# Two FFT convolutions in a written-out tile order: first-channel-group products beside other tiles, one list of spectrum slots, a ring of ten

## The chip, the core and the metric

The kernel runs on one core of a Trainium2 chip. The metric is device time in microseconds (us) from the first to the last instruction; the kernel before takes 455.67 us (median of 3 runs, 454.72 to 457.34). Six engines matter here: PE is the tensor engine, ACT the scalar engine, DVE the vector engine, POOL the GpSimd engine, SP the queue that issues nearly all transfers, and the DMA engines carry them. SBUF is the working memory, PSUM the accumulators that PE writes and that ACT or DVE must empty ("evacuate").

## The reference

Four residual layers follow one another on a 2048 x 512 activation: attention A, convolution B, attention A, convolution B. A is a sliding dilated attention (32 heads of 16, eight keys two positions apart). B is a long convolution along the sequence, with a kernel K made of complex exponentials, computed by FFT:

```python
K  = jnp.einsum("dn,dnl,dn->dl", Cc, P, dB).real     # (512, 2048)
Kf = rfft2(pad(K));  Uf = rfft2(pad(u.T))            # length 4096
Yf = Uf * Kf
y  = irfft2(Yf)[:, :, 0, :L].astype(bf16).T + u * Dskip
x  = x + _A(_layernorm(x));  x = x + _B(_layernorm(x))   # twice
```

Both B layers use the same K, so its spectrum is computed once, in the first convolution, and written to device memory for the second.

## The kernel before, in words

The program generates K on chip (`k_gen`), runs the first attention, the first convolution, the second attention and the second convolution. Only the two convolutions change.

The FFT is done by matrix products in two steps each way. The 512 channels are handled as 128 groups of four, split into two halves g = 0 and g = 1 of 64 groups each (`NG`, `DQG`). Class `FftB` has these pieces, each of which works on one PSUM tile of 128 x 1024 f32 (two of the eight banks):

- `f1` (line 697): first forward step. Sixteen half-width matmuls (line 706) fill a tile, and one evacuation writes it to `a1s`. There are eight tiles per half and source, t = 0 to 7. Sources are `ka` (the kernel K, first convolution only) and `ua` (the activation).
- `f2` (line 709): second forward step, sixteen 128 x 64 matmuls (line 713), eight tiles ("slots", ec = 0 to 7) per half and source. It reads all of `a1s` of its half.
- `k_f2` (line 716): an f2 tile of K, evacuated into a slot buffer and stored to `kf_dram` (line 729).
- `u_f2` (line 770): an f2 tile of the activation, evacuated by ACT into `ub` (line 776). `ub` has three buffers.
- `u_mult` (line 749): the spectral product of one slot, two DVE multiplications (line 757) of `ub` with the slot's spectrum kn and with its copy ks, in which real and imaginary rows are swapped. They write `t1` and `t2`.
- `i1` (line 780): first inverse step, sixteen matmuls (lines 791 and 792) that read `t1` and `t2` of a half over all eight slots, so each i1 tile needs all products of its half; the evacuation writes `z` (for g = 0 it is placed in the buffer `xnT`).
- `i2` (line 796): second inverse step, eight matmuls of 256 columns (lines 807 and 808), four tiles per half. With "dve" the residual is added by DVE (line 811); with "act" PE adds it by four more matmuls with the identity (line 806) and ACT copies; "both" splits the tile.

The spectrum copies come by DMA. In the first convolution `kf_load` (line 731) copies a slot's kn to its ks with even and odd partitions exchanged, two transfers inside SBUF. In the second it reads a slot from `kf_dram` in three transfers (lines 744 and 746), 512 KB in all, into a ring of seven slots. A slot is loaded again only after the product that used it.

The order of work in these stages is the program's order: a manual schedule is on for DVE, ACT, PE and SP, so each engine executes its instructions as they are recorded. `forward` (line 820) records in steps s: the product of the slot before, one f1 tile, and, eleven steps behind, one f2 tile. So all products come after the whole of K's spectrum, each directly after its u tile; after the eleventh of them i1 tiles of half 0 are put in between. `middle` (line 853) then records i1 of half 1 and i2 of half 0, and the main function records i2 of half 1. Which engine evacuates is decided by `evac` (line 690), a running balance: ACT is charged 0.93 and DVE 1.2 per tile, and the one with the smaller sum takes it.

PSUM for the convolutions is four tiles, two pools of two buffers (line 664), taken two and two in turn. After `middle`, `swap_psum` closes both and opens one pool of two buffers, and the other half goes to the next attention's front (transposes and key projections).

The two convolutions differ at the edges. Before the first, the list `late` of the attention (line 504) holds five pieces, among them the row statistics of `x_sb` rows 14 and 15 and the layer norm of the last rows; `forward` places one after each f1 tile. After the first, the next attention's front is recorded in the main function (lines 1312 to 1344): per block b of four row groups, `stats(b)` takes row statistics of the second channel half (four DVE instructions, line 91), `aggr`, `power` and `norm` produce `xn`, PE transposes it (line 205) into `pt`, ACT and DVE copy it to `xnT` (line 208), and `keys` project it. The statistics of the first channel half of block t are taken in `middle`, after `i2(0, t)`.

Of the kernel before, what the change touches and what calls it, by code (L numbers as in the profile page):

```python
# [20 lines left out]
P = 128  # L21
S = 2048
D = 512
# [20 lines left out]
EV = dict(act=0.93, dve=1.2)  # L44
# [96 lines left out]
class LayerA:  # L141
# [388 lines left out]

    def close_logits(self):
        self.lctx.close()
# [122 lines left out]
class FftB:  # L655


    def __init__(self, tc, nc, C, ident, w2_dram, g2_dram, kf_dram, x_sb, tag):
        self.tc, self.nc, self.C, self.ident, self.kf_dram, self.x_sb = tc, nc, C, ident, kf_dram, x_sb
        self.w2_dram, self.g2_dram = w2_dram, g2_dram  # L660
        self.tag = tag
        self.c_grp, self.c_mid, self.c_ps = ExitStack(), ExitStack(), ExitStack()
        self.grp = self.c_grp.enter_context(tc.tile_pool(name=f"b{tag}_grp", bufs=5, reuse_waits="tile"))
        self.ps = [self.c_ps.enter_context(tc.tile_pool(name=f"b{tag}_ps_{side}", bufs=2, space=PSUM, side=side))
                   for side in ("right", "left")]
        self.npt = 0
        self.load = dict(act=0.0, dve=0.0)
        self.pend = None
        g2p = self.c_grp.enter_context(tc.tile_pool(name=f"b{tag}_g2", bufs=1, reuse_waits="tile"))
        self.g2 = g2p.tile([P, 2, 16, P], BF16, name="g2_sb")  # L670
        self.S = [dict() for _ in range(NG)]

    def open_mid(self):
        tc, nc, t = self.tc, self.nc, self.tag
        nc.sync.dma_start(self.g2[:], self.g2_dram[:])
        self.kf_ring = None
        if self.ring_pool is None:
            self.ring_pool = self.c_mid.enter_context(tc.tile_pool(name=f"b{t}_kf", bufs=1, reuse_waits="tile"))
        self.ring2 = self.c_mid.enter_context(tc.tile_pool(name=f"b{t}_kf2", bufs=1, reuse_waits="tile")) if t else None
        self.nkf = 0  # L680
        self.wk = self.c_mid.enter_context(tc.tile_pool(name=f"b{t}_wk", bufs=3, reuse_waits="tile"))

# [7 lines left out]
    def evac(self, dst, src, eng=None):  # L690
        nc, load = self.nc, self.load
        if eng is None:
            eng = "act" if load["act"] + EV["act"] <= load["dve"] + EV["dve"] else "dve"
        load[eng] += EV[eng]
        (nc.scalar.copy if eng == "act" else nc.vector.tensor_copy)(dst, src)  # L695

    def f1(self, g, u, key, t):
        nc, C = self.nc, self.C
        if t == 0:
            self.S[g][key] = self.gtile("a1s", [P, P, DQG])  # L700
        a1s = self.S[g][key]
        p1 = self.ptile([P, DQT, P])
        for j in range(DQT):
            lhs = u[:, g * DQG + t * DQT + j].rearrange("p a r -> p (a r)")
            for half, m in enumerate((C["F1c"], C["F1s"])):
                nc.tensor.matmul(p1[half * 64:(half + 1) * 64, j, :], lhsT=lhs, rhs=m[:], start=True, stop=True)  # L706
        self.evac(a1s[:, :, t * DQT:(t + 1) * DQT], p1[:].rearrange("p q e -> p e q"))
# [8 lines left out]
    def k_f2(self, g, ec):  # L716
        if (g, ec) == (0, 0):
            self.nat = list(self.spare)
        elif ec == 0:
            kp2 = self.ring_pool.tile([P, 8, DQG, EC], BF16, name="kf_nat", tag="kp")  # L720
            self.kf_ring = kp2
            self.nat += [kp2[:, 4 + i] for i in range(4)]
        p2 = self.f2(g, "ka", ec)
        n = g * NEC + ec
        if n >= len(self.nat):
            self.nat.append(self.wk.tile([P, DQG, EC], BF16, name="kf_sb")[:])
        kf = self.nat[n]
        self.evac(kf, p2)
        self.nc.sync.dma_start(self.kf_dram[g, ec].rearrange("p r q e -> (p r) (q e)"), kf.rearrange("p q e -> p (q e)"))

    def kf_load(self, n):

# [7 lines left out]
        if self.kf_ring is None:  # L740
            self.kf_ring = [pool.tile([P, 4 - i, 2, DQG, EC], BF16, name=f"kf_ring{i}")
                            for i, pool in enumerate((self.ring_pool, self.ring2))]
        kc = self.kf_ring[n % 7 // 4][:, n % 7 % 4]
# [5 lines left out]
    def u_mult(self):  # L749

        if self.pend is None:
            return
        g, ec, ub = self.pend
        self.pend = None
        kn, ks = self.kf.pop(g * NEC + ec)
        for t, k in zip(self.S[g]["t"], (kn, ks)):
            self.nc.vector.tensor_tensor(t[:, :, ec * EC:(ec + 1) * EC], ub[:], k, ALU.mult)  # L757
        self.load["dve"] += 1.22
        n = g * NEC + ec
        if self.tag == 0:  # L760
            self.free += [ks] + ([kn] if n < len(self.spare) else [])
            more = len(self.free)
        else:
            more = 1
        while more and self.nkf < min(NG * NEC, n + 9):
            self.kf_load(self.nkf)
            self.nkf += 1
            more -= 1

    def u_f2(self, g, ec):  # L770
# [4 lines left out]
        ub = self.wk.tile([P, DQG, EC], BF16, name="ub")  # L775
        nc.scalar.copy(ub[:], p2)  # L776
        self.load["act"] += EV["act"]
        self.pend = (g, ec, ub)

    def i1(self, g, t, eng=None):  # L780
# [15 lines left out]
    def i2(self, g, t, eng="dve", defer=False):  # L796
# [12 lines left out]
        if n_add:  # L809
            xr = x_sb[:, t * 4:t * 4 + n_add, dsl]  # L810
            nc.vector.tensor_tensor(xr, p4[:, 0:n_add], xr, ALU.add)
            self.load["dve"] += 0.3 * n_add
        if n_add < 4:
            ev = lambda: nc.scalar.copy(x_sb[:, t * 4 + n_add:t * 4 + 4, dsl], p4[:, n_add:4])
            self.load["act"] += 0.23 * (4 - n_add)
# [4 lines left out]
    def forward(self, srcs, late=()):  # L820

        F1 = [(g, u, key, t) for key, u in srcs for g in range(NG) for t in range(NQT)]
        F2 = [(key, g, ec) for key, _ in srcs for g in range(NG) for ec in range(NEC)]
        lag = NQT + 3
        late = list(late)
        self.kf = {}
        n_u = 0
        for s in range(len(F2) + lag):
            self.u_mult()
            if s < len(F1):  # L830
                self.f1(*F1[s])
            if s > 0 and late:
                late.pop(0)()
            if s >= lag:
                key, g, ec = F2[s - lag]
                if s == max(lag, lag + len(F2) - NG * NEC - 4):
                    if self.tag == 0:
                        self.free = [self.kf_ring[:, i] for i in range(4)]
                    for n in range(self.ahead):
                        self.kf_load(n)  # L840
                    self.nkf = self.ahead
                if key == "ka":
                    self.k_f2(g, ec)
                else:
                    self.u_f2(g, ec)
                    n_u += 1
                    if n_u > NEC + 3:
                        self.i1(0, n_u - NEC - 4)
        self.u_mult()
        for t in range(NEC - 3, NQT):  # L850
            self.i1(0, t)

    def middle(self, done, eng=None, last="dve"):
        self.i1(1, 0, eng)
        self.i1(1, 1, eng)
        for t in range(NA // 4):
            if t == 3:
                self.i1(1, 6, eng)
                self.i1(1, 7, eng)
            self.i2(0, t, "dve" if t < 3 else last)  # L860
            done(t)
            if t < 2:
                self.i1(1, 2 + 2 * t, eng)
                self.i1(1, 3 + 2 * t, eng)

    def swap_psum(self):
        self.c_ps.close()
        self.c_ps = ExitStack()
        self.ps = [self.c_ps.enter_context(self.tc.tile_pool(name=f"b{self.tag}_ps2", bufs=2, space=PSUM))]
# [317 lines left out]
def kernel(  # L1187
# [93 lines left out]
    fb.free = None  # L1281
    fb.open_mid()
    with tc.manual_schedule(engines=MAN):
        fb.forward((("ka", kp), ("ua", u)), late)
# [4 lines left out]
    with tc.manual_schedule(engines=MAN):  # L1289
        fb.middle(lambda t: half_stats(nc, lnst, x_sb, t, 0), "act", "act")  # L1290
# [4 lines left out]
        def stats(b):  # L1295
            half_stats(nc, lnst, x_sb, b, 1)

# [14 lines left out]
        fb.i2(1, 0)  # L1312
# [53 lines left out]
    fb.ahead = 7  # L1366
    fb.open_mid()
    with tc.manual_schedule(engines=MAN):
        fb.forward((("ua", u),))
    fb.c_mid.close()  # L1370
    la.close()
    out_v = out.rearrange("b (p a) d -> p (b a) d", p=P)

    def store(g):
        gs = slice(g * 4 * DQG, (g + 1) * 4 * DQG)

        def rows(t):
            for a in ((t * 4, t * 4 + 2) if (g, t) == (1, 3) else (t * 4,)):
                a1 = a + (2 if (g, t) == (1, 3) else 4)
                nc.sync.dma_start(out_v[:, a:a1, gs], x_sb[:, a:a1, gs])  # L1380
        return rows

    with tc.manual_schedule(engines=MAN):
        done = store(0)
        fb.middle(done)
        done = store(1)
        for t, eng in enumerate(("dve", "act", "dve", "both")):
            fb.i2(1, t, eng)
            done(t)
# [32 lines left out]
```

## Time and profile before

| what | from the page or an answer of the trace |
|---|---|
| span | 453.2 us, 12714 instructions |
| PE busy | 354.9 us (78%), weight loads 268.0 us (59%) |
| DVE busy | 402.2 us (89%) |
| ACT busy | 326.0 us (72%) |
| transfers | 54.17 MB, mean 120 GB/s |
| mean granted PE clock | 0.980 |
| first convolution | about 213 to 286 us: DVE busy 60.5, ACT 60.7, PE 63.5 of 73.0 us |
| second convolution | about 396 to 452 us: DVE busy 42.0, ACT 40.0, PE 44.4 of 56.0 us |

Busy shares are averages over stages with different limits. In both convolutions no engine is busy all the time, and what a change of order is worth must be read from who waits for whom: an engine that waits holds back what stands behind it in its queue. Busy time of PE contains overlapping matmuls, so a busy PE isn't PE at its peak. A busy sum that is built of long runs also counts a small overlap at the seams: an ACT evacuation lasts 1.02 us, but in an unbroken run they start 0.9 to 0.93 us apart.

### The profile page before, as it was taken

The page shows a single profiled execution, that of the slowest core. Times are in us where ns is not written, and L with a number is a line of the kernel's source. Part 1 is how long each engine was busy: PE and PEld are TensorE (multiplying, and loading weights), DVE is VectorE, ACT ScalarE, POOL GpSimd, SP SyncE. Part 2 cuts the span into 40 slices and gives each one's busy share as a digit, 9 for nine tenths or more (in the row PEclk, how much of TensorE's full clock was granted, in tenths as well). Part 3 has the DMA queues.
Part 4 walks back from the last instruction along what each step waited for, and adds up shares of the span by engine and source line. Part 5 has one row for each costly group of instructions (what it writes and reads, how often), then busy time and mean ns, then how long its engine had stood idle before and what let it go on. Part 6 is the DMA issues. An engine that isn't in the chain of part 4 may idle for free.

```text
span 453.2 us, 12714 instructions
## 1 busy us (share of the span) xinstructions
PE 354.9 (78%) x5459; PEld 268.0 (59%) x5498; DVE 402.2 (89%) x558; ACT 326.0 (72%) x543; POOL 44.5 (10%) x46
## 2 busy tenths in 40 slices
PE   1000065888999989989898788999999899996885
PEld 1000034666676667767787787555657687776874
DVE  6799999999899999898897888889999999878964
ACT  5979979576555559967999886774654559699943
POOL 2000110100089300000400000000000020000000
PEclk9999997899999999999999999999999999998999
DMA  8920730121411575480266440670033053016714
GB/s 213 391 80 12 79 66 19 32 64 24 101 16 43 160 234 159 135 338 14 112 245 221 176 169 7 173 249 1 2 82 83 1 213 161 18 79 184 239 48 140
DMA packets 65354, 54.17 MB, mean 120 GB/s; under 512 B 36781, under 2 KB 53778, under 8 KB 64018
## 3 DMA queue, kind: packets, MB, share of 16 engines
q1 hardware_dynamic: 65154, 53.22, 38.8%
q8 instruction: 43, 0.70, 0.7%
q10 hardware_dynamic: 144, 0.13, 0.3%
q14 instruction: 13, 0.11, 0.1%
HBM read 30.28 MB, written 13.24 MB: 96 GB/s over the span
## 4 chain that ended last, share of the span: by engine, by line
PE 52%; ACT 20%; DVE 16%; DMA 7%; issue 3%; SPq 1%; DVEq 0%; ACTq 0%
PE po L385 9%; PE pp L219 6%; PE pq L326 6%; PE pq L162 5%; PE L L280 5%; PE pq L397 4%; PE pk L1111 4%; DVE t L757 4%; DVE pav L377 3%; ACT a1s L695 3%; DMA v_ext<-v_ext 3%; PE pb L713 2%; PE pb L706 2%; ACT ln_junk L86 2%; ACT ln_junk L81 2%
## 5 line engine op out<-in xcount | busy, mean ns | idle before, releaser
L377 DVE TENSOR_TENSOR pav<-attn,v_ext 128x4096 bf16<-128x4096 bf16 x32 | 72.7, 2282 | 0.5 <-DMA v_ext<-v_ext 0.5
L273 DVE TENSOR_TENSOR prod<-qT,kT_ext 128x4096 bf16<-128x4096 bf16 x29 | 66.2, 2299 | 1.1 <-ACT qT L164 0.6
L385 PEld LDWEIGHTS <-pav 128*128 128x128 bf16 x1024 | 58.6, 98 | 13.0 <-DVE pav L377 9.4
L385 PE MATMUL po<-ident,pav 128*128 128x128 bf16 x1024 | 62.5, 219 | 4.8 <-DVE pav L377 4.8
L205 PE MATMUL pt<-ident,x_blk 128*128 128x128 bf16 x64 | 5.6, 241 | 45.1 <-ACT x_blk L136 45.1
L791 PE MATMUL pb<-Wp,t 128*128 128x128 bf16 x256 | 31.0, 219 | 7.0 <-DVE t L757 4.6
L219 PE MATMUL pp<-xnT,kT_ext 128*128 128x512 bf16 x124 | 31.1, 393 | 4.0 <-ACT xnT L208 3.8
L776 ACT CAST ub<-pb 128x1024 bf16<-128x1024 f32 x32 | 32.0, 1039 | 2.5 <-DVE t L757 2.5
L119 POOL TENSOR_TENSOR ln_rstd<-ln_rstd,ln_mh 128x4 f32<-128x4 f32 x6 | 10.0, 1658 | 229.0 <-DVE ln_rstd L118 207.0
L1111 PE MATMUL pk<-B_t,A_t 128*64 128x84 bf16 (+1 forms) x512 | 27.0, 217 | 6.8 <-issue 3.5
L713 PE MATMUL pb<-a1s,w_sb 128*128 128x64 bf16 x768 | 31.0, 199 | 1.2 <-ACT ub L776 1.0
L328 ACT CAST v_ext<-pq 128x512 bf16<-128x512 f32 x32 | 18.7, 586 | 18.2 <-PE pq L326 18.0
L205 PEld LDWEIGHTS <-x_blk 128*128 128x128 bf16 x64 | 4.4, 108 | 46.3 <-ACT x_blk L136 46.0
L792 PE MATMUL pb<-WpJ,t 128*128 128x128 bf16 x256 | 30.6, 219 | 1.5 <-DVE t L757 1.5
L280 PEld LDWEIGHTS <-prod 128*128 128x128 bf16 x928 | 27.3, 96 | 7.4 <-DVE prod L273 1.5
L1111 PEld LDWEIGHTS <-A_t 128*64 128x64 bf16 (+1 forms) x512 | 24.7, 115 | 10.0 <-issue 5.9
L326 PE MATMUL pq<-wv,xnT 128*128 128x512 bf16 x119 | 30.3, 379 | 0.4
L162 PE MATMUL pq<-xnT,kT_ext 128*128 128x512 bf16 x121 | 30.0, 379 | 0.4 <-issue 0.2
L388 ACT CAST oT<-po 128x512 bf16<-128x512 f32 x32 | 18.5, 578 | 16.2 <-PE po L385 16.1
L397 PE MATMUL pq<-wop,oT 128*128 128x512 bf16 x110 | 29.3, 379 | 0.9
L713 PEld LDWEIGHTS <-w_sb 128*128 128x128 bf16 x768 | 27.5, 102 | 4.2 <-issue 1.6
L695 ACT CAST a1s<-pb 128x1024 bf16<-128x1024 f32 x28 | 27.4, 1027 | 2.4 <-PE pb L706 2.2
(221 smaller groups left out, 883.9 us busy)
## 6 DMA issues: line engine op xcount, KB each, us to landing
w_sb<-w_dram SPq DMA_DIRECT2D x8, 1024.0 KB
w_dram<-w_zero SPq DMA_DIRECT2D x1, 4096.0 KB
kf_ring<-kf_dram SPq DMA_DIRECT2D x16, 256.0 KB
kf_ring<-kf_dram SPq DMA_DIRECT2D x32, 128.0 KB
v_ext<-v_ext SPq DMA_DIRECT2D x4, 784.0 KB
x_blk<-in_A_x_dram SPq DMA_DIRECT2D x4, 512.0 KB
kT_ext<-in_A_wqkv_dram SPq DMA_DIRECT2D x4, 512.0 KB
x_sb<-in_A_x_dram SPq DMA_DIRECT2D x4, 512.0 KB
```

Of the source, the lines that this page charges most:

```text
L162: nc.tensor.matmul(pq[:], lhsT=self.wqk[:, dt, ft * P:(ft + 1) * P], rhs=self.xnT[:, dt, q * 512:(q + 1) * 512], start=(dt == 0), stop=(dt ...
L219: nc.tensor.matmul(pp[:], lhsT=self.wqk[:, dt, D + ft * P: D + (ft + 1) * P], rhs=self.xnT[:, dt, b * 512:(b + 1) * 512], start=(dt == 0), ...
L273: nc.vector.tensor_tensor(pr, self.qT[q][:, ft].unsqueeze(1).to_broadcast([P, W, 4, P]), kap, ALU.mult)
L280: self.nc.tensor.matmul(L[:, al, w, ft * 8:(ft + 1) * 8], lhsT=pr[:, w, al, :], rhs=self.c["ind8"][:], start=(ft == 0 and w == 0 and al % ...
L326: nc.tensor.matmul(pp[:], lhsT=xnT[:, dt, a * P:(a + 1) * P], rhs=wv[:, dt, :], start=(dt == 0), stop=(dt == NDT - 1))
L377: nc.vector.tensor_tensor(pv[:], attn[:, n % 4].unsqueeze(2).to_broadcast([P, W, DH, H]), vap, ALU.mult)
L385: nc.tensor.matmul(po[:, ft, :], lhsT=pvf[:, w, ft * P:(ft + 1) * P], rhs=ident[:], start=(w == 0 and ft == 0), stop=(w == W - 1), skip_gr ...
L397: nc.tensor.matmul(pw[:], lhsT=oT[:, ftp, :], rhs=wo[:, ftp, :], start=False, stop=(ftp == NDT - 1))
L695: (nc.scalar.copy if eng == "act" else nc.vector.tensor_copy)(dst, src)
L713: nc.tensor.matmul(p2[:, j, :], lhsT=self.w2[:, ec * EC + j, :], rhs=a1s[:, ec * EC + j, :], start=True, stop=True)
L776: nc.scalar.copy(ub[:], p2)
L1111: nc.tensor.matmul(o, lhsT=lhs, rhs=Bt[:, ri, c * CH + ql].rearrange("p b g -> p (b g)"), start=(not half and j % 4 == 0 and ri == 0), sto ...
```

## The change

`forward` and `middle` are replaced by `run`, which reads a string of tokens, one per tile, and records the tile with the engine named in it. Capital K and U are f1 tiles of the kernel and of the activation, k an f2 tile of K, u an f2 tile of the activation, m the product of a slot, y an i1 tile and z an i2 tile; A, D or B after the letter names ACT, DVE or both. The n-th token of a letter is tile n, of half g = n // 8 (n // 4 for z). The purpose is that products of one half stand beside evacuations of other tiles of the next, that i1 tiles stand where PE and ACT have room, and that a fixed division between ACT and DVE replaces the running balance.

```diff
-EV = dict(act=0.93, dve=1.2)
+ORDER0 = """
+KA KD KA KD KA KA KD KA KD KA KD kA KD KA KA kD kA kD kA UA KD UA UA UD UA kD UA
+UA UD KA UA kD u kD m u u u kA m UA m UD UA u kA m kD u UA u m UA m
+UD m UA kA u kD kD u kA u m m kA m u u yD yA m u u m u m yA u yA
+yA m m yA m yA yD yD yD yD yD zD yA yA zD yA yA zD zD zD
+"""
+ORDER1 = """
+UD UA UA UD UA UA UD UA UD UA UD u UD u m UA u u m UA m u u UA m UD m
+u u m m m u u m u m m u u m u m m u yA yA yA m u yA yA yA yA
+m yD yA yD yD yA zD yD yA zD yA yA zD zD zD zD zA zB
+"""
```

The slots of the first convolution come from one list `free` (nine spare buffers, three more, and eight once the K input is used up); a product gives back both of its buffers. `pump` issues spectrum copies up to `ahead` slots beyond the last product, 4 in the first convolution and 10 in the second, where the ring gets three more slots: one in the unused end of the `w2` buffer and two in the buffers of the attention's queries.

```diff
+    def ring_extra(self):
+        n = 2 * DQG * EC
+        rest = [self.w2_rest[:, 0:n]] + [self.keep.tile([P, n], BF16, name=f"kx_{i}", tag="qT", bufs=2)[:] for i in range(2)]
...
+    def pump(self):
+        while self.nkf < min(self.nk, self.nm + self.ahead):
+            self.kf_load(self.nkf)
+            self.nkf += 1
...
-        kc = self.kf_ring[n % 7 // 4][:, n % 7 % 4]
+        kc = self.ring[n % len(self.ring)]
...
-        if self.tag == 0:
-            self.free += [ks] + ([kn] if n < len(self.spare) else [])
...
-        while more and self.nkf < min(NG * NEC, n + 9):
-            self.kf_load(self.nkf)
...
+        self.nm += 1
         if self.tag == 0:
-            more = len(self.free)
...
+            self.free += [kn, ks]
+        self.pump()
...
     def swap_psum(self):
         self.c_ps.close()
-        self.c_ps = ExitStack()
-        self.ps = [self.c_ps.enter_context(self.tc.tile_pool(name=f"b{self.tag}_ps2", bufs=2, space=PSUM))]
+        self.ps = self.ps[1:]
```

In the main function the first-half statistics after the first convolution's `i2` stay in the list for blocks 0 and 1 only; those of blocks 2 and 3 move into the next attention's front, where `stats(2)` and `stats(3)` now take both halves. `i2(1, 0)` becomes the last token of ORDER0. The second convolution's stores are issued from the list after each z tile, as before.

```diff
-        fb.forward((("ka", kp), ("ua", u)), late)
+        def half(g, t):
+            if g == 0 and t < 2:
+                half_stats(nc, lnst, x_sb, t, 0)
+
+        fb.run(ORDER0, u, half, kp, late)
...
-        fb.middle(lambda t: half_stats(nc, lnst, x_sb, t, 0), "act", "act")
...
         def stats(b):
             half_stats(nc, lnst, x_sb, b, 1)
+            if b > 1:
+                half_stats(nc, lnst, x_sb, b, 0)
...
-    fb.ahead = 7
+    fb.ring, fb.extra = [], la.ring_extra()
+    fb.ahead = 10
...
-        fb.forward((("ua", u),))
...
+        fb.run(ORDER1, u, store)
```

## The prediction

> **What bounds the kernel now.** I read the page first (vector engine, DVE, 89% busy; scalar engine, ACT, 72%; tensor engine, PE, 78%: no single wall), then the busy table by stretch for the two convolutions, the only stages the change touches. Columns: busy us and instruction count of PE, PEld, DVE, ACT and POOL, then PE clock, DMA share, GB/s.
>
> ```profile
> core 0: us, PE busy (x) PEld busy (x) DVE busy (x) ACT busy (x) POOL busy (x), PEclk, DMA share, GB/s
> 212.80:282.30 69.50, 60.28 (x1325) 53.67 (x1323) 57.57 (x83) 58.50 (x65) 6.37 (x9) 0.98 0.43 154
> 282.30:303.00 20.70, 20.16 (x147) 11.93 (x149) 17.16 (x60) 15.32 (x28) 0.00 (x0) 1.00 0.69 199
> 399.20:433.00 33.80, 26.45 (x642) 24.33 (x641) 28.85 (x40) 29.99 (x32) 0.00 (x0) 0.95 0.48 143
> 433.00:450.00 17.00, 15.07 (x197) 13.85 (x197) 10.30 (x9) 7.47 (x8) 0.00 (x0) 1.00 0.34 102
> ```
>
> The first convolution takes 69.5 us (first DVE evacuation to the end of `i2(1, 0)`) with DVE and ACT each busy about 58: both lose 11 to 12 us to each other. The second takes 33.8 us to its last spectrum product and 17.0 us for the inverse, there with PE at 15.1. The waits around the first convolution name the gaps (waiter, releaser, us, times, longest):
>
> ```profile
> DVE a1s L695 <- PE pb L706: 2.6, 3, 1.6
> DVE t L757 <- ACT ub L776: 2.2, 3, 1.3
> DVE x_sb L811 <- PE pb L808: 1.7, 1, 1.7
> DVE t L757 <- DMA kf_nat<-kf_nat: 1.5, 1, 1.5
> DVE ln_bn L91 <- ACT x_sb L814: 1.5, 1, 1.5
> ```
>
> The chain of waits of the second (start, us, what) ends its forward half on a transfer:
>
> ```profile
> 424.12 0.33 SPq L744
> 424.50 4.74 DMA kf_ring<-kf_dram
> 429.36 1.29 DVE t L757 x2
> ...
> 431.70 1.29 DVE t L757 x2
> ```
>
> The product of slot 14 waits for its spectrum, slot 15 follows, and every g = 1 inverse tile waits for slot 15. Prices of back-to-back work, from the timeline of that stretch (start, us, engine line; a run of n):
>
> ```profile
> 399.96 6.61 ACT L695 CAST a1s<-pb 128x1024 bf16<-128x1024 f32 x7 [0.85 <-PE pb L706]
> 400.41 5.89 DVE L695 CAST a1s<-pb 128x1024 bf16<-128x1024 f32 x5 [1.33 <-PE pb L706]
> 414.99 9.72 DVE L757 TENSOR_TENSOR t<-ub,kf_ring 128x1024 bf16<-128x1024 bf16 x16 [0.81 <-ACT ub L776]
> ```
>
> I take 0.92 us for an ACT evacuation (6.61 less one of 1.02, over 6, gives 0.93; five `ub` copies in 4.68 give 0.915), 1.15 for a DVE one (5.89 less 1.22, over 4, is 1.17; four in 4.64 earlier give 1.14), 1.21 for a product pair (9.72 over 8).
>
> **What the Trainium skill says.** "PSUM — Partial Sum Buffer", section Engine vs sequencer instructions: the queues of ScalarE, VectorE and GpSimd are strict FIFO. So a written order is binding: an instruction that waits holds all behind it. The trace agrees: the 1.5 us above stop DVE while other tiles stand ready. The same page, Specifications: 8 banks of 2 KiB per partition; a convolution tile of 1024 f32 takes two, so four tiles fill PSUM and PE is never more than four evacuations ahead. "VectorE: DVE Perf Modes", Why PSUM operands drop a tier: an fp32 PSUM source runs at 1x; the trace agrees (1.22 us for a 1024-element evacuation, 0.685 for a bf16 SBUF product), so evacuations belong on ACT and each one given to DVE is dear. "DMA: Bandwidth & Descriptors", Anatomy of one DMA: some 2 us fixed per transfer. The trace has more: a slot swap issued at 255.19 is used at 259.57, 4.4 us later.
>
> **First convolution, order.** Work is the same, its division is not. The old greedy `evac` gave DVE 22 evacuations (14 + 3 + 2 + 2 + 1 by group) and 4 residual adds; ORDER0 gives it 25 and 5, while two of the four row-statistics groups (1.41 us each) leave. DVE: 57.6 + 3 x 1.15 + 1.2 - 2.8 = 59.4 us. ACT: four evacuations fewer, 58.5 - 3.7 = 54.8. So DVE becomes the bound, and the gain is in gaps. What stays of DVE's gaps: 1.0 + 1.6 us at the head (rows 14 and 15 of `x_sb`, PSUM of the attention), which nothing moves. Along the list I added ACT and DVE separately: before the first `m`, DVE has 14 evacuations (16.1) and 2.2 of late statistics from 212.9 with 2.6 idle, so 233.8; ACT has 20 (18.3) and 0.4 from 216.1, so 234.8: DVE waits 1.0, and behind it stand only products and evacuations that ACT's lag holds back anyway. For every later `m`, the ACT sum at its `u` is 0 to 1.5 us below the DVE sum before it: no further wait. `ub` has three buffers; for u10 to u15 the freeing product ends about 1 us or more ahead. PE needs some 0.5 us for a forward tile and 0.89 and 0.87 for the inverse ones (16 matmuls at 0.056, 8 at 0.109), 52 us in all, under DVE. Best case: 59.4 + 2.6 + 1.0 = 63.0, 6.5 us less than 69.5.
>
> Unknown is what four PSUM tiles and two nearly full engines lose. Lower bound 0. Upper: in the pure evacuation stretch of before (224 to 240) DVE waited 0.5 us four times in 14 evacuations; on 25 that is 3.6. Add up to 0.8 for transfers: a swap is now issued four products ahead, and for m14 and m15 the list leaves 3.6 us where 4.4 were measured; behind m14 on DVE stand m15 and five y evacuations, and all g = 1 tiles of PE wait for m15. I take 1.9 of 4.4: the forward tiles are interleaved with products, which need no PSUM. So the stage gains 4.6.
>
> **The moved statistics.** `stats(2)` and `stats(3)` now do both halves, eight instructions each, in the key stage of the next layer. There DVE has no slack:
>
> ```profile
> 290.47 1.40 DVE L91 BATCH_NORM_STATS2 ln_bn<-x_sb 128x6 f32<-128x256 bf16 x4
> 291.79 0.67 DVE L208 COPY xnT<-pt 128x1024 bf16<-128x1024 bf16 x1
> 292.38 0.41 DVE L1301 BATCH_NORM_AGGREGATE ln_ag<-ln_bn 128x2 f32<-128x12 f32 x4
> 293.47 0.16 DVE L126 SCALAR_TENSOR_TENSOR ln_nb<-ln_ag,ln_rstd 128x4 f32<-128x4 f32 x1 [0.68 <-ACT ln_rstd L97]
> 293.67 1.38 DVE L138 TENSOR_SCALAR xn<-x_sb,ln_rstd,ln_nb 128x512 bf16<-128x512 bf16 x4
> 294.97 1.39 DVE L91 BATCH_NORM_STATS2 ln_bn<-x_sb 128x6 f32<-128x256 bf16 x4
> ```
>
> `xn` ends at 295.05 and PE transposes it at 295.06; DVE's block (290.47 to 294.97, 4.5 us) is as long as PE's. Queued behind the longer statistics are the `xnT` copy that the next keys read and the `xn` that the next transposes read. So each of two blocks is 1.3 us longer: +2.6. Net of the first convolution: -2.0.
>
> **Second convolution.** The ring of ten preloads ten slots instead of seven. The three new ones stand in the DMA queue behind the `w2` loads of the attention stage, where DMA is nearly idle (share 0.01 in 380 to 390); I cost them at nothing. Nine loads used to follow products, from 408.84 to 428.4, 2.1 us each; six remain, 408 + 6 x 2.1 = 421, landing by 424: off the path, provided m15 isn't before. Without it, DVE sets m15: 7 evacuations (8.05) and 16 pairs (19.4) from 399.96 is 427.4; ACT to u15 has 28 (9 UA, 16 u, three yA), 25.6 from 400.45, and about 1.4 of waiting for `ub` buffers, 427.5, for which the last pair waits 1.0; one more wait of 0.3 at m2. m15 ends at 428.7, against 433.0: 4.3 us earlier. Behind m15 the work is as before: 8 tiles of i1 and 8 of i2, 8 x 0.89 + 8 x 0.87 + 6 identity matmuls x 0.11 = 14.8 us of PE, which was 15.3 from 433.05 to 448.36. DVE has four evacuations, six adds and a half there, 12.4: hidden under PE. Putting g = 0's y tiles ahead of m15 gains nothing more, they already were. I take 0.6 off for small waits: -3.7.
>
> **Free edits.** One slot list, dictionaries in place of a pending tuple, PSUM pools closed elsewhere, stores issued from the same call: no instruction added; the same matmuls and evacuations stay. Cost zero.
>
> Sum: -2.0 - 3.7 = -5.7; 455.67 - 5.7 = 450.0 us.
>
> **Rivals.** (a) The statistics are hidden: if `i2(1, 1..3)` or the first transposes leave a hole for them, 2.6 come back: 447.4, and 445 if there are no stalls either. For: other columns of the wait list have gaps of 0.6 us per block (DVE on ACT); against: that wait is in series with them. Chance 0.13. (b) The first convolution gains nothing, since DVE carries more work and PSUM couples the engines: only the ring counts, 455.67 - 3.7 = 452.0. For: both engines over 85% of the new length. Chance 0.22. (c) Slower: stores of late spectra now share the queue with swaps, the four-ahead swap takes 9 us instead of 4.4, and a product comes every 2.25 us instead of the 1.75 that the list plans (15 in some 26 us): 12 x 0.5 = 6 us. First convolution -4.6 + 6 + 2.6 = +4; the second loses all but 1 because its extra slots come late: 458.7. Against: 204 GB/s in 236 to 262 leaves room. Chance 0.06. (d) Half of each: gains of 1 and 1, 453.7. Chance 0.06.
>
> **Numbers.** My forecast has 0.53. Best case 6.5 - 2.6 + 4.3 = 8.2, 447.5; with (a) 445. The range 446 to 455 leaves out the end of (a) and (c). Under 453.4 is faster: 0.53 + 0.13 + 0.22, less 0.05 for spread of measurement, 0.83; within 0.5% 0.11; slower 0.06.
>
> **What would show it.** Right: `i2(1, 0)` ends near 277.7 with DVE above 90% until then; 2.7 us of statistics before each of two `xnT` copies and those transposes late by 1.3 and 2.6; no DVE wait for `kf_ring`; the last product pair ends 29 to 30 us after that stage's first evacuation (33 before); the inverse tail still 15 us of PE. Wrong: DVE waiting for a swap more than 1 us in all, PE idle in the key stage without a longer block, or the tail of the second convolution shorter than 15 us.

## The result and the profile after

The changed kernel takes 449.96 us (median of four runs, 448.71 to 450.50), the kernel before, run beside it, 455.20 us. The ratio is 0.9874, 95% interval 0.9833 to 0.9916: faster by about 1.3%, and 450.0 us were forecast. In a later comparison the same kernel took 448.91 us (ratio 0.9886, 0.9847 to 0.9925).

The busy table by stretch of the changed kernel, with the columns of the table of before; the four stretches are the first convolution's list, the key stage behind it, the forward half of the second convolution and its inverse:

```profile
core 0: us, PE busy (x) PEld busy (x) DVE busy (x) ACT busy (x) POOL busy (x), PEclk, DMA share, GB/s
212.30:277.10 64.80, 57.27 (x1329) 52.40 (x1327) 58.73 (x80) 53.69 (x61) 6.37 (x9) 1.00 0.46 165
277.10:300.80 23.70, 20.31 (x143) 11.34 (x144) 19.83 (x68) 15.49 (x29) 0.00 (x0) 1.00 0.69 201
...
398.40:427.90 29.50, 24.53 (x616) 22.18 (x611) 27.57 (x39) 27.72 (x30) 0.00 (x0) 1.00 0.36 110
427.90:445.00 17.10, 15.59 (x212) 14.55 (x208) 12.51 (x12) 8.84 (x10) 0.00 (x0) 1.00 0.31 94
```

The first list is 4.7 us shorter, DVE is busy 58.73 of its 64.8 us (91%; 83% before) and ACT has lost 4.8 us of work. The key stage is longer. The forward half of the second convolution is shorter, with DVE and ACT at 93 and 94%; its inverse is as it was.

The waits of DVE in the first list (waiter, releaser, us, times, longest), the four largest (the second has 0.3 us ahead of the list):

```profile
DVE a1s L709 <- PE pb L720: 2.4, 3, 1.6
DVE ln_bn L89 <- ACT x_sb L411: 1.3, 2, 1.0
DVE t L767 <- DMA kn<-w_sb: 0.8, 1, 0.8
DVE kf_sb L709 <- PE pb L727: 0.6, 1, 0.6
```

With the smaller ones they make 6.1 us. Before, the same view added up to 12.0. Gone are the waits for ACT's `ub` (2.2), for PE before the residual add (1.7), for ACT's `x_sb` (1.5) and about half of those for a slot swap (1.7, now 0.8).

Two places of DVE's timeline (start, us, engine line, tiles):

```profile
285.25 2.70 DVE L101 BATCH_NORM_STATS2 ln_bn<-x_sb 128x6 f32<-128x256 bf16 x8
287.87 0.67 DVE L218 COPY xnT<-pt 128x1024 bf16<-128x1024 bf16 x1
...
426.64 1.29 DVE L767 TENSOR_TENSOR t<-ub,kf_ring 128x1024 bf16<-128x1024 bf16 x2 [1.21 <-ACT ub L779]
```

The first two lines are the moved statistics, eight instructions in place of four, and the `xnT` copy queued behind them. The chain of waits now runs through `ln_bn` in this stage, at 285.33 and at 290.97 (2.62 us each); before, most of the chain in this stage was PE's transposes and key projections. The third line is the last product pair: it waits for ACT's `ub`, no longer for a spectrum.

For the experiments I cut each profile at the same marks: the first list (first DVE evacuation to the end of `i2(1, 0)`), the key stage (to the end of the last `xn`), the second attention (from the first `prod`, which in every kernel starts 4.26 us after that, to the first evacuation of the second convolution), the products (to the end of the last pair) and the tail (to the end of the last residual add on DVE). In us:

| kernel | list | key stage | attention | products | tail |
|---|---|---|---|---|---|
| before | 69.39 | 17.17 | 96.25 | 33.02 | 16.15 |
| after | 64.73 | 19.54 | 97.62 | 29.45 | 16.29 |
| difference | -4.66 | +2.37 | +1.37 | -3.57 | +0.14 |

With 0.56 us less ahead of the list the differences make the 4.91 us between the two profiles at the last residual add.

### The profile page after: what moved, and what is told of

Its sections match the earlier page's. It is cut to its first block, busy times and chain, and to the rows that moved or that the text cites. A ratio compares the mean times of both kernels' runs of the same rounds, so it can differ in the third digit from the quotient of the medians.

```text
span 448.7 us, 12704 instructions
## 1 busy us (share of the span) xinstructions
PE 350.1 (78%) x5455; PEld 264.8 (59%) x5494; DVE 407.2 (91%) x563; ACT 320.1 (71%) x538; POOL 44.5 (10%) x46
## 4 chain that ended last, share of the span: by engine, by line
PE 46%; ACT 25%; DVE 15%; DMA 7%; SPq 3%; issue 3%; ACTq 0%; DVEq 0%
PE po L395 7%; PE pq L336 6%; PE pq L172 5%; PE pp L229 5%; PE L L290 4%; ACT a1s L709 4%; PE pk L1092 4%; PE pq L407 4%; ACT ub L779 3%; ACT ln_junk L96 2%; SPq L1162 2%; DVE ln_bn L101 2%; DVE pav L387 2%; ACT ln_junk L91 2%; ACT x_blk L146 2%
## 5 line engine op out<-in xcount | busy, mean ns | idle before, releaser
L395 PE MATMUL po<-ident,pav 128*128 128x128 bf16 x1024 | 64.1, 222 | 5.1 <-DVE pav L387 5.1
L395 PEld LDWEIGHTS <-pav 128*128 128x128 bf16 x1024 | 60.2, 99 | 13.1 <-DVE pav L387 9.0
L779 ACT CAST ub<-pb 128x1024 bf16<-128x1024 f32 x32 | 33.0, 1089 | 2.0 <-DVE t L767 1.8
L727 PE MATMUL pb<-a1s,w_sb 128*128 128x64 bf16 x768 | 27.1, 193 | 5.7 <-ACT ub L779 3.5
L709 ACT CAST a1s<-pb 128x1024 bf16<-128x1024 f32 x30 | 29.3, 1079 | 1.3 <-PE pb L720 1.3
L1092 PE MATMUL pk<-B_t,A_t 128*64 128x84 bf16 (+1 forms) x512 | 24.7, 208 | 6.9 <-issue 3.0
L727 PEld LDWEIGHTS <-w_sb 128*128 128x128 bf16 x768 | 24.7, 98 | 8.1 <-issue 7.0
L1092 PEld LDWEIGHTS <-A_t 128*64 128x64 bf16 (+1 forms) x512 | 22.6, 108 | 10.0 <-issue 6.0
```

Of the source, the lines that this page charges most:

```text
L395: nc.tensor.matmul(po[:, ft, :], lhsT=pvf[:, w, ft * P:(ft + 1) * P], rhs=ident[:], start=(w == 0 and ft == 0), stop=(w == W - 1), skip_gr ...
L709: (self.nc.scalar.copy if eng == "act" else self.nc.vector.tensor_copy)(dst, src)
L727: nc.tensor.matmul(p2[:, j, :], lhsT=self.w2[:, ec * EC + j, :], rhs=a1s[:, ec * EC + j, :], start=True, stop=True)
L1092: nc.tensor.matmul(o, lhsT=lhs, rhs=Bt[:, ri, c * CH + ql].rearrange("p b g -> p (b g)"), start=(not half and j % 4 == 0 and ri == 0), sto ...
```

## The experiments

Expectations are quoted as they stood on record. Times in one group have the same kernel before beside them: 454.4 us for the first four, 454.95 for the next four, 455.4 for the last four. Single profiles differ by a us or two for a reason that comes out below, so I read the mechanism from the stages and only the direction from the total.

**One convolution at a time.** First, the new first convolution with the second in its old order and with the ring of seven.

```diff
 ORDER1 = """
-UD UA UA UD UA UA UD UA UD UA UD u UD u m UA u u m UA m u u UA m UD m
-u u m m m u u m u m m u u m u m m u yA yA yA m u yA yA yA yA
-m yD yA yD yD yA zD yD yA zD yA yA zD zD zD zD zA zB
+UA UD UA UD UA UD UA UA UD UA UD UA u m UA u m UD u m UA u m UA u m
+u m u m u m u m u m u m u yA m u yD m u yA m u yA m u yD
+m yA yA yA yD yA zD yA yA zD yA yD zD yA yA zD zD zA zD zB
...
-    fb.ring, fb.extra = [], la.ring_extra()
-    fb.ahead = 10
+    fb.ring, fb.extra = [], []
+    fb.ahead = 7
```

> The first convolution in the new order with its moved statistics, the second in the order of before with a ring of seven (the old order written as a token list). Theory, the two convolutions gain separately: the first gives 2.2 us net (its list ends 4.6 us sooner, the key stage gives 2.4 back), so 455.2 - 2.2 = 453.0 us; in the trace the list spans 64.7 us and the second convolution 33 us from its first evacuation to its last product, with a wait on the ring again. Rival, the whole gain is the second convolution's: 455.2 us.

Measured: 452.54 us, ratio 0.9963 (0.9940 to 0.9986). List 64.69, key stage 19.54, as in the changed kernel; products 32.67. The first convolution, with its slot list, brings about 2 us, as forecast (-4.7 and +2.4).

Then the new second convolution alone, with the first in its old tile order and old division, and all statistics in the list. The slot list and the swaps issued four ahead stay.

```diff
 ORDER0 = """
-KA KD KA KD KA KA KD KA KD KA KD kA KD KA KA kD kA kD kA UA KD UA UA UD UA kD UA
...
+KA KD KA KD KA KD KA KA KD KA KD KA kD KA kA KD kA KD kA KD kA UD kA UA kD UA
+kD UA kD UA kA UD kA UD kA UD kA UD kA UA kD UA kD UA u m UA u m UD u m
+UA u m UA u m u m u m u m u m u m u m u yA m u yD m u yA
+m u yA m u yA m yA yD yA yA yA zD yA yA zD yA yA zD yA yA zA zD
...
-            if g == 0 and t < 2:
+            if g == 0:
...
-            if b > 1:
-                half_stats(nc, lnst, x_sb, b, 0)
```

> The first convolution in the order of before with all statistics in it, the second in the new order with the ring of ten. Theory: 455.2 - 3.6 = 451.6 us; the last product ends 29.4 us after the stage's first evacuation, the first convolution takes 69.4 us. Rival, the second convolution was long in the profile of before only because of a slow-clock episode in it (410 to 415 us): 453.5 us or more.

Measured: 449.28 us, ratio 0.9899 (0.9856 to 0.9942), 2.3 us better than expected. The products take 29.46, as in the changed kernel. But the list takes 67.37, 2.0 us less than before although its order is the old one: the waits for swaps, 1.7 us in the profile of before, are absent. So the slot list, with the swaps issued four ahead, brings something without the new order, as far as one profile of each shows. In total this kernel can't be told from the changed one (449.96 and 448.91 us). The list's busy table and its DVE waits that the changed kernel doesn't have:

```profile
212.81:280.18 67.37, 61.21 (x1339) 54.98 (x1337) 57.29 (x83) 59.05 (x65) 6.37 (x9) 0.97 0.44 158
```

```profile
DVE t L767 <- ACT ub L779: 2.2, 3, 1.3
DVE x_sb L812 <- PE pb L809: 1.7, 1, 1.7
DVE ln_bn L101 <- ACT x_sb L814: 1.5, 1, 1.5
```

**Ring and order of the second convolution, apart.** The changed kernel with the ring of seven (of the first diff only the hunk on the ring):

> The changed kernel with a ring of seven in place of ten (no extra slots, seven loaded ahead). Theory, transfers set the last product of the old ring: nine loads follow the products at 2.1 us each, from about 8.5 us after the first evacuation, so the last product ends some 31.5 to 32 us after it instead of 29.4: 449.96 + 2.3 = 452.3 us, with a DVE wait on the ring of 2 us or more. Rival, the order alone gave the gain: 450 us.

Measured: 450.60 us, ratio 0.9907 (0.9872 to 0.9942). The products take 32.66 us, 3.2 more than with the ring of ten and just what the old order takes with a ring of seven (32.67). DVE waits for the ring at five products:

```profile
DVE t L767 <- DMA kf_ring<-kf_dram: 3.0, 5, 1.1
```

The changed kernel with the old ORDER1 and the ring of ten (the other hunk):

> The changed kernel with the second convolution in the order of before, ring of ten kept. Theory: without the wait for the ring the old order loses 1.1 us of DVE idle and what followed from it, but keeps its lockstep of u tile and product: last product after 31.5 us, 451.9 us. If the ring alone were the cause: 450 us. If the order alone: 453.5 us.

Measured: 450.71 us, ratio 0.9907 (0.9880 to 0.9938). Products 31.29, 1.4 less than the old order with seven, and no wait for the ring. So of the 3.2 us between the old pair and the new one the ring alone brings 1.4, the order alone nothing, and both together all of it. The new order asks for spectra earlier than seven buffers can bring them. With ten, the old order is held by something else: DVE has eight evacuations ahead of its last pair instead of seven (1.2 us more), starts 0.45 us after ACT, and waits 2.0 us for ACT's `u` instead of 1.2. The totals were 1 to 2 us below what I expected of both runs; the key figures are the products.

This also answers the rival named with the new second convolution, a slow clock. All three profiles with the old order there (before and two here) have PE at half clock for 3.4 us in this stage, those with the new order don't. But in this stretch or just behind it DVE waited for ACT's `u` only 0.8 us with seven buffers and 0.3 with ten, so the clock explains at most that much of the 3.2 us.

**The statistics back in the list**, for all four blocks (the last two hunks of the second diff), beside the changed kernel unaltered:

> The changed kernel again, unaltered, beside the three that follow. All theories: 449.96 us; first list 64.7 us, key stage 19.5, second convolution 29.5 from first evacuation to last product. If the swap of a slot is near its limit, its wait differs from run to run (0.8 to 3.8 us so far) and the list with it.

> The row statistics of blocks 2 and 3 back in the first list, as before the change; the rest as changed. Theory, DVE is the bound in the list and in the key stage alike, so 2 x 1.4 us only change places: list 67.5 us, key stage 17.2, total 450.3 us against 450.0. Rival, they are hidden in the key stage: list 67.5, key stage 19.5 all the same or a shorter one by under 1 us, total 452.5 us.

Measured: unaltered 448.91 us (list 64.97, key stage 19.54, attention 95.88); statistics back 450.76 us, ratio 0.9900 (0.9863 to 0.9938), list 67.49, key stage 18.67. The list pays 2.5 us. The key stage gets back only 0.9, not 2.4: two lines, of PE's timeline and of DVE's, show why.

```profile
283.57 1.87 PE L215 MATMUL pt<-ident,xn 128*128 128x128 bf16 x16 [2.67 <-DVE xn L148]
```

```profile
291.51 0.69 DVE L218 COPY xnT<-pt 128x1024 bf16<-128x1024 bf16 x1 [1.29 <-PE pt L215]
```

PE idles 2.67 us for the first `xn`, then works at a granted clock of 0.66 from 285 to 290, and DVE waits 1.29 us for a transpose: that is most of the 1.5 us by which this key stage exceeds 17.17. The kernel with only the second convolution new, which also has all statistics in the list, shows the same: a PE gap of 1.75 us, then half clock, and a key stage of 18.68.

This run also says what the tile order itself is worth, for it differs from the second kernel of this section only in ORDER0. Its list:

```profile
213.15:280.64 67.49, 58.99 (x1344) 53.76 (x1341) 61.51 (x87) 53.96 (x61) 6.37 (x9) 1.00 0.45 158
```

67.49 us against 67.37 in the old order. DVE has 4.2 us more to do (61.51 against 57.29) and waits 4.3 us less (6.0 against 10.3 by the view of waits). The new order takes DVE's waits out, and the division written into it fills the room with DVE work. (0.7 us of its waits are for a slot swap, of which the old order has none here.)

**Taking work off DVE.** If DVE sets the first list, giving ACT two of the five inverse evacuations in a row must shorten it by about their sum:

```diff
-yA m m yA m yA yD yD yD yD yD zD yA yA zD yA yA zD zD zD
+yA m m yA m yA yD yA yD yA yD zD yA yA zD yA yA zD zD zD
```

> The first list with two of its five consecutive DVE inverse evacuations (tiles 8 and 10) given to ACT, which idles 3.8 us there. Theory, DVE bounds the end of the list: two evacuations fewer are 2.3 us, of which PE's own pace (0.89 us a tile) leaves 1.8; list 62.9 us, total 448.2 us. Rival, four PSUM tiles or PE already set this end: list 64.5, total 450 us.

Measured: 446.99 us, ratio 0.9839 (0.9793 to 0.9885). List 63.40, 1.3 to 1.6 less than the two profiles of the changed kernel. But 0.4 to 0.6 us of that is a shorter wait for a swap (0.43 us here, 0.81 and 1.05 there). DVE has 2.0 us less to do, and a new wait, for PE's inverse tiles, takes half of it back:

```profile
DVE z L709 <- PE pb L793: 1.1, 2, 0.6
```

So the edit itself brings 0.9 us, half of the 1.8 forecast: the rival's PE is close behind DVE.

And the wait for a swap, removed by issuing the copies six slots ahead in place of four (`fb.ahead = 6`):

> In the first convolution slot copies are issued six products ahead instead of four. Theory, the wait of a product for its swapped slot is latency, so it disappears: DVE waits 0 for it, list 63.9 us or less, total 449.2 us or less. Rival, the transfer queue itself is full there (stores and swaps in turn): the wait stays at 0.8 us or more and the total at 450 us.

Measured: 446.63 us, ratio 0.9848 (0.9806 to 0.9890). No wait for a swap; list 63.94, less by 1.03 than in the unaltered run of the same group, where that wait was 1.04.

**Together.** Both edits at once:

> The changed kernel with both edits at once: the inverse tiles alternate between VectorE and ScalarE in place of five on VectorE, and spectrum copies are issued six slots ahead. Theory (VectorE is the bound of the first list, and the swap wait is a separate term): the list shortens by 1.6 from the first and by 0.4 to 0.8 from the second, to 62.6 to 63.0 us (64.7 in the changed kernel), without a wait for a swap; total near 446.0 us, the moved statistics still in the key stage (19.5 us). Rival (with less work on VectorE the end of the list hangs on TensorE and its PSUM tiles): the list stays at 63.4 and the total at 446.8 us, no better than either edit alone.

Three of its four runs took 502 to 1545 us (the profiled one had a granted clock of 0.75 from 60 us on), so only the fourth, 446.87 us, can be read; it decides nothing. The next kernel holds both edits too, and answers for the list. It moves two `xnT` copies of the key stage from DVE to ACT:

```diff
-            pt = la.front_t(b + 1, ("act", "dve"), True)
+            pt = la.front_t(b + 1, ("act", "act" if b < 2 else "dve"), True)
```

> As the last, and in the key stage the second half of the transposed rows of blocks 2 and 3 is copied by ScalarE in place of VectorE, so VectorE gets two copies of 0.67 us less in the two blocks that carry the moved statistics. Theory (VectorE's block of 5.6 us is what that stage waits for): the stage shortens from 19.5 us by up to 2 x 0.67 = 1.3, to 18.2 to 18.6, total near 445.0 us. Rival (the copies wait behind key evacuations on ScalarE and hold TensorE's transposes): 19.5 us or more, total 446.0 us or more.

Measured: 445.28 us, ratio 0.9813 (0.9752 to 0.9874). List 63.00, no wait for a swap: at the upper end of what both edits were to give (62.6 to 63.0; 63.4 by the rival), and 0.94 less than with the swaps six ahead alone, which had no swap wait either. Key stage 18.43, 1.1 less. In DVE's timeline the copy of 0.67 us is gone from behind the statistics:

```profile
281.58 2.71 DVE L101 BATCH_NORM_STATS2 ln_bn<-x_sb 128x6 f32<-128x256 bf16 x8
284.20 0.41 DVE L1286 BATCH_NORM_AGGREGATE ln_ag<-ln_bn 128x2 f32<-128x12 f32 x4
```

Both edits, with one z evacuation more on ACT (`zD zA zD` at the end) and the statistics of block 2 back in the list:

> As the one with both edits, with one more evacuation of the inverse's second step on ScalarE (z of rows 3), and the first-half statistics of block 2 back in the list, so only those of block 3 stand in the key stage. Theory (both stages are bound by VectorE, so 1.4 us of statistics cost the list what they no longer cost the key stage, unless VectorE is relieved there, which the moved evacuation of 1.2 us does): the list 62.8 to 63.4 us, the key stage 18.2 to 18.4, together 1.0 less, total near 445.0 us. Rival (the list ends on TensorE or ScalarE once VectorE is relieved): the list 64.0 or more, total 446.0 us.

Measured: 446.34 us, ratio 0.9803 (0.9737 to 0.9869); list 63.30, key stage 18.40, as the theory had it; the total is nearer the rival's 446.0 than the theory's 445.0, with runs from 443.94 to 447.39. And with the copy of the remaining long block on ACT too:

> As the last, with the copy of block 2's or 3's second half (the one block that still carries moved statistics) on ScalarE as well. Theory: the key stage another 0.6 us shorter, near 17.7 us, the list 62.8 to 63.4, total near 444.5 us, 2.4% under the kernel before. Rival: as above, no gain from the copy, 445.0 us; if ScalarE becomes the bound, 446.0 us or more.

Measured: 446.56 us, ratio 0.9825 (0.9766 to 0.9885). The key stage is the shortest of these, 17.80, but the list took 66.99 in this profile, and the total is 2 us over the theory's. DVE's timeline shows a chain of three losses:

```profile
257.55 1.29 DVE L767 TENSOR_TENSOR t<-ub,kn 128x1024 bf16<-128x1024 bf16 x2 [0.67 <-DMA kn<-kn]
...
261.43 0.69 DVE L767 TENSOR_TENSOR t<-ub,kf_sb 128x1024 bf16<-128x1024 bf16 x1 [1.39 <-DMA kf_sb<-kf_sb]
...
264.55 1.22 DVE L709 CAST z<-pb 128x1024 bf16<-128x1024 f32 x1 [1.29 <-PE pb L793]
267.54 1.22 DVE L709 CAST z<-pb 128x1024 bf16<-128x1024 f32 x1 [1.76 <-PE pb L793]
```

The swaps came late although issued six ahead; the last product of the half came late; PE, which needs it, idled 1.85 us, and its clock was then 0.50 for some 3.4 us, so that DVE waited twice more. Six ahead doesn't exclude a late swap; of the profiles above with six ahead, this is the only one that has it. The version with the copies on ACT has the lowest median of all that ran, 10 us under before and 3.6 under the unaltered changed kernel (of another group); its interval overlaps with those of the other variants, so their order among each other is not settled.

## Why the prediction was right, and where it was not

**The first list: right in size.** Forecast 64.9 us (63.0 and an allowance of 1.9), measured 64.73. DVE's work was forecast as 59.4 and is 58.73; its gaps as 5.5 and are 6.1. The end of `i2(1, 0)` was forecast near 277.7 and is 277.06, on a list that began 0.56 us earlier. Within the gaps one step failed: the wait of 1.0 us of the first product for ACT's `u` does not occur. In its place stand waits for a tile of PE of about 1.9 us beyond the head's 1.6, in the stretches of K's second step and of evacuations, 0.5 for a late row statistic of ACT, and 0.8 for a swap, the upper end of what was allowed. That DVE is the bound is shown from the other side, but only for the first 0.9 us: with two evacuations (2.0 us) less on DVE the list is 0.9 us shorter, swap waits apart, and then DVE waits for PE. One reading of the profile before was wrong: DVE and ACT don't lose their 11 to 12 us "to each other". Of DVE's waits there 4.7 us were for ACT, 5.3 for PE and 1.7 for transfers.

**What the 4.7 us are made of was not separated.** The prediction put them under "First convolution, order". The runs split them: about 2.0 us come with the slot list, in the old order (a difference that rests on swap waits, which vary from profile to profile), 2.5 to 2.8 us are statistics that only moved to the key stage, and the tile order gives nothing, since it costs DVE as much work as it saves it in waits. The prediction had the slot list among the "Free edits", at cost zero, and expected of the order some 1.8 us beside the 2.8 of the statistics. So a gain that was not foreseen stands where one that was foreseen is missing: that the list came out right to 0.2 us is in part luck. Rival (b), a first convolution that gains nothing, was thus right about the order and its reason (DVE carries more work), and wrong about the stage.

**The statistics: right.** +2.6 forecast, +2.37 measured, and the chain of waits runs through them. Rival (a), hidden statistics, falls: taking a copy off DVE in that stage, or one block's statistics, shortened it at once by 1.1 us, and by another 0.6 with the last copy. What the prediction didn't see is what the move is for. Left in the list, they delay the first `xn` and PE idles 2.67 us at the head of the key stage; with them back, list and key stage together took 86.16 us against 84.51 in the unaltered run beside it. The medians differ by 1.85 us the same way, though their intervals overlap. Nearly all of the difference in the profiles is the 1.5 us that half clock cost behind PE's gap: by this sum the move would neither gain nor lose without it. What is shown to pay in this change is therefore the slot list and the second convolution.

**The second convolution: right in size.** Forecast -3.7, measured -3.57: last pair 29.45 us after the first evacuation, no wait for the ring, tail unchanged at 16.29 against 16.15. The three extra loads cost nothing that shows: attention stages without a clock episode took 95.9 to 96.7 us with them, 96.25 before, 96.68 with a ring of seven. But the prediction's account begins with the ring, and rival (b) says that "only the ring counts": alone, with the old order, it gave 1.4 of the 3.2 us. The rest needed the new order as well.

**The swap rival (c)** had the right place and the wrong size: at four slots ahead swaps do stop DVE, by 0.4 to 3.8 us in the profiles of the new order, and nowhere near the 6 that it needed. The prediction's own sign of being wrong, more than 1 us of swap waits, did not show in the profile of after (0.8), but it did in three of the four later profiles of this list (0.8, 1.0, 1.3, 3.8): that wait was underrated.

**The sum.** List, key stage, products and tail give -4.66 + 2.37 - 3.57 + 0.14 = -5.72, forecast -5.7. The profile of after then loses 1.37 us in the second attention, which the change doesn't touch. The chain of waits shows the same 32 matmuls in both kernels, before:

```profile
352.66 2.21 DVE pav L377
354.88 0.05 issue
354.92 1.96 PE po L385 x32
```

and after:

```profile
349.76 2.21 DVE pav L387
351.97 0.05 issue
352.02 3.54 PE po L395 x32
```

1.58 us more, at a granted clock of 0.50. In the unaltered kernel of the next group the clock stayed at 1.00 there, and the stage took 95.88 us. So this part belongs to the run, not to the change, and no step of the forecast had it.

## What to carry to other kernels

When an order is rewritten, set up two sums for the fullest engine, its waits and its work: an order that removes 4.3 us of waiting and hands the engine 4.2 us of work gains nothing until the division is made again. A deeper prefetch and an order that asks earlier are one change in two parts; here each alone gave less than half of both. And where work must be moved out of a full stage, look at which engine falls idle behind it: the same statistics cost about as much in either stage (2.5 and 2.4 us), but left in the first they had PE idle for 2.67 us, half clock followed, and that cost 1.5 us.

## What the runs showed of the hardware that I had not expected

The granted clock of PE falls to 0.50 for some 3.4 us after PE has been idle for a short time. Between 205 and 435 us there are 13 such episodes in 13 profiles (all of this case but the one of 502 us): each begins in the last 0.5 us of an idle gap of PE of 1.25 to 2.67 us, or up to 2.1 us behind it. None stands behind shorter gaps alone; one of 1.17 us near 220 us, in eleven profiles, was never followed by one. Longer ones are not always: the old order's wait of 1.84 us for an `a1s` evacuation, once in either convolution, was followed by half clock each of the five times that it appears; the 1.25 us before `po` near 350 us in four of 13 profiles; three of 1.27 to 1.54 us, and gaps of 1.98 and 2.33 us ahead of the second convolution's inverse, not at all. The new order has neither of the two gaps of 1.84 us, and the clock of both convolutions reads 1.00 after, 0.98 and 0.95 before. No run changes the gap alone, so it is not shown that it is the cause, only that half clock followed the one of 1.84 us five times of five.

The Trainium skill, "TensorE: Matmul & The Clock Gate", section What's actually happening, fits in kind: half clock after an idle window, full clock again after some 3.4 us of activity, and a window that runs freely, not in step with the kernel. It gives about 3.4 us of idleness as what it takes; here 1.25 to 2.67 us were enough at times, and the measurement decides. How the window counts is not shown by these runs. What an episode cost depends on what waits for PE: 1.58 us at `po`, about 1.5 in the key stage, some 2 us in the list of the last variant, at most 0.8 in the old order's second convolution.

What a slot swap costs isn't constant either: at the same four slots ahead, DVE lost 0.8, 1.0, 0.8, 1.3 and 3.8 us to swaps in five profiles of the same first list, and at six ahead, in lists that differ by an evacuation or two, nothing in three and 2.1 us in a fourth.
